# Block 0's second 256 rows of x, transposed by DMA instead of TensorE

## Chip, cores and metric

The kernel runs on one core of a Trainium2 chip. The metric is device microseconds (us) of one execution; the median of 8 runs of the kernel before is 290.55 us (289.83 to 290.69).

## What is computed

A two-layer dense block with a squared ReLU between the layers, all in bf16:

```
B, S, D, F = 1, 2048, 576, 4608
h = einsum("bsd,df->bsf", x, w1) + b1
r = where(h > 0, h, 0)
h = r * r
out = einsum("bsf,fd->bsd", h, w2) + b2
```

## The kernel before

The 2048 rows of x are four blocks of 512. The first layer wants x transposed (D on the partitions), and w1's columns are cut into 36 tiles of 128, so the hidden layer of one block is 36 tiles of 128x512, each summed in a PSUM bank, passed through ReLU with bias on ACT (L193) and squared on DVE (L195). The second layer (from L315) runs after all four blocks and is not touched.

For blocks 1 to 3 the transposed x comes straight from memory by DMA transposes (`load_xT`, L270), and one step of the first layer (`a_step`, L212) makes two tiles by 18 matmuls of half the array's rows. Block 0 begins differently, since TensorE would otherwise have nothing to do. Its x is loaded as plain rows, 128 at a time (`load_x`, L92, named x0 to x3 here, on SP's queue), and its first six tiles of w1 come in four chunks of 128 rows (`load_quad`, L95, named q0 to q3, on ACT's queue) and a rest of 64 rows (`load_rest`, L104). `transpose_tile` (L174) turns pieces of x on TensorE into a PSUM bank, and ACT or DVE copies them into `xT[0]`. `full_mm(j, n, c)` (L226) multiplies chunk c into six PSUM banks for the n*128 rows that begin at row 128*j: six matmuls of 128 or 256 columns each. The written order, L219 to L253, weaves 20 transposes and 13 calls of `full_mm` so that a matmul is there while the next piece of x or w1 is on its way.

After that come b1's transpose (L255), six matmuls on the rest of w1 (L260), and then the steps of the first layer for block 0 (L299), beginning with step 3. Its weights, and those of the steps after it, were put in SP's queue behind x and the rest of w1 (L117 to L119): two loads for every one, two or four steps, in the order of use. The next transposes (L275) stand behind these.

`manual_schedule` keeps the program's order on every engine. Two things are inserted by the program: `issue_at_barrier` (L123) lifts those first DMAs of SP and ACT that wait for nothing into the start-up block, the first two of each queue ahead of its drain and the others behind it. And each DMA on SP or ACT uses one of eight semaphores in turn; so a DMA is issued only once the DMA eight places earlier, of the two queues together, has landed. The first reuse is by `load_rest`; it waits for q0.

Of the kernel before, what the change touches and what calls it, by code (L numbers as in the profile page):

```python
# [17 lines left out]
def kernel(  # L18
# [9 lines left out]
    nc = tc.nc  # L28
    P = 128
    H = 64  # L30
    x2 = x.flatten_outer_dims()
    out2 = out.flatten_outer_dims()
    S, D = x2.shape
# [6 lines left out]
    NC = D // P  # L40
    NH = D // H
    DM = NC * P
    SB = 512
    NSB = S // SB
    RT = SB // P
    HALF = SB // 2
# [23 lines left out]
    def early(n):  # L70
        at[0] += n
        assert at[0] <= NFT * D
        return w2_sb[:, at[0] - n:at[0]]


    xT = [early(XW).rearrange("p (w s) -> p w s", s=SB) for b in range(NSB - 1)]
    xT3 = xpool.tile([P, NH, SB], BF16, name="xT3", tag="xT3")
    xT.append(xT3[:])
    xs = early(RT * D).rearrange("p (j c) -> p j c", c=D)
    qn = early(NC * G * P).rearrange("p (c f) -> p c f", c=NC)  # L80
    qr = early(GP * P)
    pairs = [(i, GP + i) for i in range(GP)] + [(G + i, G + NJ - GP + i) for i in range(NJ - GP)]
# [9 lines left out]
    def load_x(eng, j):  # L92
        eng.dma_start(out=xs[:, j, :], in_=x_view[:, j, :])

    def load_quad(eng, c):  # L95
        eng.dma_start(out=qn[:, c, :], in_=w1[c * P:(c + 1) * P, 0:G * P])
# [9 lines left out]

    b1T = const.tile([P, NFT], FP32, name="b1T")
    warm = const.tile([P, 1], FP32, name="warm")
    for j in range(RT):
        load_x(nc.sync, j)  # L110
        load_quad(nc.scalar, j)
    nc.scalar.activation(out=warm[:], in_=nc.const_aps.tensor(1.0, [P, 1], FP32), func=ACT.Relu)  # L112
    for h in range(2):
        load_rest(nc.sync, h)
# [8 lines left out]
    def issue_at_barrier(nc):  # L123
        entry, body = nc.main_func.blocks[:2]
        for engine in (mybir.EngineType.SP, mybir.EngineType.Activation):
            mine = [i for i in body.instructions if i.engine == engine and not isinstance(i, mybir.InstNoOp)]
            n = 0
            while isinstance(mine[n], mybir.InstDMACopy) and not mine[n].has_wait():
                n += 1
            assert n >= RT  # L130
            for k, i in enumerate(mine[:n]):
                wanted = mybir.InstDrain if k < 2 else mybir.InstEventSemaphore
                at = next(k for k, i in enumerate(entry.instructions) if i.engine == engine and isinstance(i, wanted))
                body.instructions.remove(i)
                entry.instructions.insert(at, i)

    nc.at_finalize(issue_at_barrier)


# [28 lines left out]
    def copy_psum(eng, dst, src):  # L168
        if eng is nc.scalar:
            nc.scalar.copy(out=dst, in_=src)  # L170
        else:
            nc.vector.tensor_copy(out=dst, in_=src)  # L172

    def transpose_tile(j, c, n, eng):  # L174
        cols = slice(j * P, (j + 1) * P)
        tp = psum.tile([P, n, P], BF16, name="tp", tag="bank")
        for k in range(n):
            d0 = (c + k) * P if c < NC else D - P
            nc.tensor.transpose(tp[:, k, :], xs[:, j, d0:d0 + P], ident[:])  # L179
        c0 = c if c < NC else 7  # L180
        copy_psum(eng, xT[0][:, c0:c0 + n, cols], tp[:])
        if c == NC:
            copy_psum(eng, xT[0][0:H, 8, cols], tp[H:P, 0, :])
# [35 lines left out]
    V, A = nc.vector, nc.scalar  # L219
# [6 lines left out]
    def full_mm(j, n, c):  # L226
        cols = slice(j * P, (j + n) * P)
        for q in range(G):
            nc.tensor.matmul(bk0[q][:, cols], lhsT=qn[:, c, q * P:(q + 1) * P], rhs=xT[0][:, c, cols],  # L229
                             start=(j == 0 and c == 0), stop=False, skip_group_check=True)  # L230
# [3 lines left out]
    transpose_tile(1, 2, 2, A)  # L234
    full_mm(0, 1, 1)
    full_mm(1, 1, 0)
    transpose_tile(2, 0, 2, V)
    full_mm(1, 1, 1)
    transpose_tile(2, 2, 2, A)
    full_mm(0, 2, 2)  # L240
    transpose_tile(3, 0, 2, V)
    full_mm(2, 1, 0)
    full_mm(2, 1, 1)
    transpose_tile(3, 2, 2, A)
    full_mm(2, 1, 2)
    transpose_tile(1, NC, 1, V)
    full_mm(0, 2, 3)
    transpose_tile(2, NC, 1, V)
    full_mm(3, 1, 0)
    full_mm(3, 1, 1)  # L250
    transpose_tile(3, NC, 1, A)
    full_mm(3, 1, 2)
    full_mm(2, 2, 3)  # L253
    b1T_ps = psum.tile([P, P], BF16, name="b1T_ps", tag="bank")
    nc.tensor.transpose(b1T_ps[:], b1_rows[:], ident[:])  # L255
    nc.vector.tensor_copy(out=b1T[:], in_=b1T_ps[:, 0:NFT])
    for i in range(GP):
        for h in range(2):
# [117 lines left out]
```

## Time and profile before

| | |
|---|---|
| median of 8 runs | 290.55 us |
| the profiled execution | 290.01 us, of which the span of the profile is 288.2 us |
| PE busy | 284.5 us (99%) |
| DVE, ACT busy | 79.8 us (28%), 95.5 us (33%) |
| first step of the first layer begins (L209) | 11.14 us |
| second layer begins (L322) | 145.33 us |

Times in the profile are counted from the start of its span. The 1.8 us between span and execution are outside of what it shows. "SPq" and "ACTq" are the instruction queues that issue DMAs; the time shown for such a row is that of issuing, and "to landing" counts from the start of issue to the last of 16 completions. The names in a row leave numbers out: `w_sb` is the memory of w2, which holds `xT`, the plain x and the first chunks of w1 until w2 is loaded.

### The profile page before, as it was taken

The numbers are of one execution on the slowest core, as the hardware profiler recorded it, in microseconds if no ns is written. First come the engines' busy times: TensorE is split into PE (matmuls) and PEld (weight loads), VectorE is DVE, ScalarE is ACT, GpSimd is POOL, SyncE is SP. The second block draws the span as 40 slices with busy tenths as digits, with TensorE's granted clock in tenths as the row PEclk, the third lists the DMA queues.
The fourth block names the chain that finished last, engine by engine and source line by source line (L and its number), as shares of the span: only waits on it lengthen the run. The fifth ranks groups of instructions, "written<-read, shape, count | busy, mean of one in ns | idle before, by whom it ended". The sixth has DMA issues, their size and how long they took to land.

```text
span 288.2 us, 4883 instructions
## 1 busy us (share of the span) xinstructions
PE 284.5 (99%) x2097; PEld 135.1 (47%) x2108; DVE 79.8 (28%) x200; ACT 95.5 (33%) x154; POOL 1.5 (1%) x8
## 2 busy tenths in 40 slices
PE   9999999999999999999999999999999999999996
PEld 6644444444444444444445444444444444444454
DVE  2654444544444444444420011111100011111111
ACT  3676766666676666667620000000000000000000
POOL 2000000000000000000000000000000000000000
PEclk9999999999999999999999999999999999999999
DMA  8999999930400005200000000000000000000000
GB/s 242 182 202 204 196 140 227 281 105 0 125 0 2 1 2 156 92 0 2 0 3 18 20 20 20 23 20 9 12 23 20 20 20 23 20 20 22 23 20 20
DMA packets 35381, 18.31 MB, mean 64 GB/s; under 512 B 22804, under 2 KB 35360, under 8 KB 35360
## 3 DMA queue, kind: packets, MB, share of 16 engines
q1 hardware_dynamic: 34752, 17.21, 26.8%
q10 hardware_dynamic: 576, 0.79, 0.8%
q8 instruction: 16, 0.26, 0.4%
q14 instruction: 5, 0.04, 0.1%
q0 software_dynamic: 32, 0.01, 0.0%
HBM read 12.23 MB, written 2.36 MB: 51 GB/s over the span
## 4 chain that ended last, share of the span: by engine, by line
PE 97%; ACT 1%; issue 0%; DVE 0%
PE ph L209 47%; PE po L336 43%; PE pc L322 5%; PE ph L229 2%; ACT L112 0%; PE tp L179 0%; PE ph L260 0%; DVE o_sb L338 0%; ACT w_sb L170 0%; ACT warm L112 0%; PE b1T_ps L255 0%
## 5 line engine op out<-in xcount | busy, mean ns | idle before, releaser
L193 ACT ACTIVATE r<-ph,b1T 128x512 bf16<-128x512 f32 x144 | 90.7, 686 | 45.8 <-PE ph L209 45.0
L209 PE MATMUL ph<-w_sb,w1h 64*128 64x512 bf16 x918 | 99.2, 376 | 0.0
L209 PEld LDWEIGHTS <-w1h 64*128 64x128 bf16 x1242 | 60.4, 94 | 73.6
L336 PE MATMUL po<-w_sb,hT 128*128 128x512 bf16 x423 | 92.9, 379 | 0.5
L336 PEld LDWEIGHTS <-hT 128*128 128x128 bf16 x432 | 42.2, 98 | 51.2 <-issue 0.4
L195 DVE TENSOR_TENSOR hT<-r 128x512 bf16<-128x512 bf16 x108 | 45.8, 425 | 52.3 <-ACT r L193 51.9
L338 DVE TENSOR_TENSOR o_sb<-po,b_bc 128x512 bf16<-128x512 f32 (+2 forms) x17 | 11.2, 660 | 116.7 <-PE po L336 109.7
L209 PE MATMUL ph<-xT,w1h 64*128 64x512 bf16 x324 | 35.1, 376 | 0.0
L336 PE MATMUL po<-w_sb,w1h 128*128 128x512 bf16 (+2 forms) x178 | 31.2, 336 | 0.1
L336 PEld LDWEIGHTS <-w1h 128*128 128x128 bf16 x180 | 16.2, 98 | 15.3
L195 DVE TENSOR_TENSOR w1h<-r 128x512 bf16<-128x512 bf16 x36 | 15.3, 425 | 19.6 <-ACT r L193 19.6
L322 PE MATMUL pc<-hT,w_sb 128*64 128x512 bf16 x108 | 15.7, 379 | 0.0
L322 PEld LDWEIGHTS <-w_sb 128*64 128x64 bf16 x144 | 8.1, 110 | 7.6 <-issue 0.4
L322 PE MATMUL pc<-w1h,w_sb 128*64 128x512 bf16 x36 | 7.9, 379 | 0.0
L229 PE MATMUL ph<-w_sb 128*128 128x128 bf16 (+1 forms) x78 | 6.9, 246 | 0.0
L229 PEld LDWEIGHTS <-w_sb 128*128 128x128 bf16 x78 | 5.9, 106 | 0.2
L324 ACT ACTIVATE oc<-pc,b2T 128x512 bf16<-128x512 f32 x2 | 1.4, 687 | 13.7 <-PE pc L322 13.7
L332 DVE COPY o_sb<-oc 128x64 bf16<-128x64 bf16 x16 | 2.8, 172 | 9.2 <-DMA oc<-oc 9.2
L172 DVE COPY w_sb<-tp 128x128 bf16<-128x128 bf16 (+2 forms) x11 | 2.6, 242 | 6.4 <-PE tp L179 6.3
L170 ACT COPY w_sb<-tp 128x256 bf16<-128x256 bf16 (+2 forms) x6 | 2.0, 334 | 4.5 <-PE tp L179 4.5
L179 PE MATMUL tp<-ident,w_sb 128*128 128x128 bf16 x20 | 3.1, 259 | 0.1
L166 PE MATMUL wps<-one 128*128 128x512 bf16 x5 | 2.3, 629 | 0.4 <-DVE one L141 0.4
(26 smaller groups left out, 10.6 us busy)
## 6 DMA issues: line engine op xcount, KB each, us to landing
w_sb<-in_w_dram SPq DMA_DIRECT2D x2, 1728.0 KB, 8.9
out_dram<-o_sb SPq DMA_DIRECT2D x15, 144.0 KB, 1.8
w1h<-in_w_dram SPq DMA_DIRECT2D x14, 144.0 KB, 4.4
w_sb<-in_w_dram SPq DMA_DIRECT2D x2, 864.0 KB, 7.4
w1h<-in_w_dram SPq DMA_DIRECT2D x4, 288.0 KB, 6.4
w1h<-in_w_dram SPq DMA_DIRECT2D x2, 576.0 KB, 10.2
w1h<-in_w_dram SPq DMA_DIRECT2D x2, 432.0 KB, 6.9
w_sb<-in_w_dram ACTq DMA_DIRECT2D x4, 192.0 KB, 3.9
```

The lines of the kernel that those rows point to most:

```text
L166: nc.tensor.matmul(wps[:], lhsT=ones[:, 0:P], rhs=ones[:], start=(i == 0), stop=(i == NWARM - 1))
L170: nc.scalar.copy(out=dst, in_=src)
L172: nc.vector.tensor_copy(out=dst, in_=src)
L179: nc.tensor.transpose(tp[:, k, :], xs[:, j, d0:d0 + P], ident[:])
L193: nc.scalar.activation(out=r[:], in_=bk[:], func=ACT.Relu, bias=b1T[:, ft:ft + 1], scale=1.0)
L195: nc.vector.tensor_tensor(out=hT_of(b, ft), in0=r3, in1=r3, op=ALU.mult)
L209: nc.tensor.matmul(bk[h][:], lhsT=w1h[rows, c, j * P:(j + 1) * P], rhs=xT[b][rows, place(h, c), :], start=(i == 0), stop=(i == NH - 1))
L229: nc.tensor.matmul(bk0[q][:, cols], lhsT=qn[:, c, q * P:(q + 1) * P], rhs=xT[0][:, c, cols], start=(j == 0 and c == 0), stop=False, skip_g ...
L322: nc.tensor.matmul(pc[h * H:(h + 1) * H, :], lhsT=w2(ft, DM, D), rhs=hT_of(2 * pr + h, ft), start=(ft == 0), stop=(ft == NFT - 1))
L332: nc.vector.tensor_copy(out=o_sb[:, DM:D], in_=o_tr[pr][:, jj, h * H:(h + 1) * H])
L336: nc.tensor.matmul(po[:, 0:e - a], lhsT=hT_of(b, ft)[:, jj, :], rhs=w2(ft, a, e), start=(ft == 0), stop=(ft == NFT - 1))
L338: nc.vector.tensor_tensor(out=o_sb[:, a:e], in0=po[:, 0:e - a], in1=b2_bc[:, a:e], op=ALU.add)
```

## The change

x2 and x3 are no longer loaded as plain rows. In their place in SP's queue stand two DMA transposes from memory, t0 and t1 here: t0 brings the 256 rows of x2 and x3 for the first 512 columns of D into `xT[0]`, t1 their last 128 columns, of which 64 are new and lie in the upper half of place 7; a copy on DVE puts those into place 8 as well. The 10 transposes of these rows on TensorE are gone, with their copies on DVE and ACT. The order of the matmuls is written anew: all four chunks meet the first 256 rows, and then each of the four chunks meets the second 256 rows in six matmuls of 256 columns. `issue_at_barrier` lifts transposes too; as before, SP's first four DMAs are lifted, two of them behind the drain.

```diff
-    xs = early(RT * D).rearrange("p (j c) -> p j c", c=D)
+    xs = early(RT // 2 * D).rearrange("p (j c) -> p j c", c=D)
...
-    for j in range(RT):
+    for j in range(2):
         load_x(nc.sync, j)
-        load_quad(nc.scalar, j)
+    for c in range(NC):
+        load_quad(nc.scalar, c)
+    late = slice(HALF, SB)
+    nc.sync.dma_start_transpose(out=xT[0][:, 0:NC, late], in_=x2[late, 0:DM])
+    nc.sync.dma_start_transpose(out=xT[0][:, 7, late], in_=x2[late, D - P:D])
...
-            while isinstance(mine[n], mybir.InstDMACopy) and not mine[n].has_wait():
+            while isinstance(mine[n], (mybir.InstDMACopy, mybir.InstDmaTransposeAnt)) and not mine[n].has_wait():
...
     full_mm(1, 1, 0)
-    transpose_tile(2, 0, 2, V)
     full_mm(1, 1, 1)
-    transpose_tile(2, 2, 2, A)
+    transpose_tile(1, NC, 1, V)
     full_mm(0, 2, 2)
-    transpose_tile(3, 0, 2, V)
-    full_mm(2, 1, 0)
-    full_mm(2, 1, 1)
-    transpose_tile(3, 2, 2, A)
-    full_mm(2, 1, 2)
-    transpose_tile(1, NC, 1, V)
     full_mm(0, 2, 3)
-    transpose_tile(2, NC, 1, V)
-    full_mm(3, 1, 0)
-    full_mm(3, 1, 1)
-    transpose_tile(3, NC, 1, A)
-    full_mm(3, 1, 2)
-    full_mm(2, 2, 3)
+    for c in range(NC):
+        full_mm(2, 2, c)
     b1T_ps = psum.tile([P, P], BF16, name="b1T_ps", tag="bank")
     nc.tensor.transpose(b1T_ps[:], b1_rows[:], ident[:])
+    nc.vector.tensor_copy(out=xT[0][0:H, 8, late], in_=xT[0][H:P, 7, late])
     nc.vector.tensor_copy(out=b1T[:], in_=b1T_ps[:, 0:NFT])
```

## The prediction

> **What bounds the kernel now.** I read the busy shares first, then the chain that ended last, then the first 12 us in order of time, then the DMAs behind them.
>
> ```profile
> PE 284.5 (99%) x2097; PEld 135.1 (47%) x2108; DVE 79.8 (28%) x200; ACT 95.5 (33%) x154; POOL 1.5 (1%) x8
> ...
> PE 97%; ACT 1%; issue 0%; DVE 0%
> ```
>
> The first line gives busy time by engine, the second the chain of waits by engine. TensorE is never free and is the chain, so a microsecond counts if it comes off TensorE's own stream, and only then. The chain in order of time shows the stretch that the change touches (start, length, what):
>
> ```profile
> 3.48 0.20 ACT warm L112
> 3.68 0.27 ACT w_sb L170
> 3.95 0.04 issue
> 3.99 0.58 PE tp L179 x4
> 4.58 0.99 PE ph L229 x12
> 5.57 0.11 PE tp L179 x2
> ...
> 9.50 0.99 PE ph L229 x12
> 10.49 0.06 PE b1T_ps L255
> 10.55 0.75 PE ph L260 x6
> 11.30 134.03 PE ph L209 x1242
> ```
>
> From 3.99 on nothing but TensorE stands in it: transposes (tp) and matmuls (ph) follow each other without a gap up to 145 us. In the starts of single matmuls, 128 columns take 107 ns until 5.12 and 56 ns afterwards, 256 columns 109 ns. All ten removed transposes run after 5.12.
>
> The timeline of the queues gives the issues (start, length), and the lines of single DMAs the landings:
>
> ```profile
> 0.00 1.92 SPq L93 DMA_DIRECT2D w_sb<-in_x_dram  x4
> ...
> 0.12 1.95 ACTq L96 DMA_DIRECT2D w_sb<-in_w_dram  x4
> ...
> 2.91 1.19 SPq L105 DMA_DIRECT2D w_sb<-in_w_dram  x2
> ...
> 4.14 16.57 SPq L100 DMA_DIRECT2D w1h<-in_w_dram  x20
> ```
>
> q3 is issued at 1.61 and lands 5.2 later, at 6.8; q2 at 1.25, landing at 5.5; x2 lands at 5.2, x3 at 6.5. The first use of x3 begins at 6.51, so x3 just comes in time now, and q3 has 1.1 us to spare before its first use at 7.90. The DMAs are not idle (window, PE, PEld, DVE, ACT, POOL busy, clock, DMA share, GB/s):
>
> ```profile
> 0.00:5.00 5.00, 4.54 (x26) 2.84 (x27) 1.16 (x6) 2.12 (x4) 1.51 (x8) 1.00 0.79 247
> 5.00:11.10 6.10, 6.10 (x87) 5.43 (x86) 1.97 (x8) 1.47 (x5) 0.00 (x0) 1.00 1.04 213
> ...
> 40.00:42.00 2.00, 2.00 (x22) 0.88 (x18) 1.49 (x5) 1.27 (x2) 0.00 (x0) 1.00 0.87 55
> ...
> 44.00:46.00 2.00, 2.00 (x22) 0.92 (x20) 0.91 (x3) 1.27 (x2) 0.00 (x0) 1.00 0.99 207
> ```
>
> The last two are stretches in which DMA transposes ran almost alone: 207 GB/s in one, 55 in the other.
>
> What is known of issuing a transpose (min, median, max in ns):
>
> ```profile
> L326 SPq DMA_TRANSPOSE oc<-oc x2: 1191/1198/1206, 154.0 to 161.7; - x2
> ...
> L273 SPq DMA_TRANSPOSE w_sb<-in_x_dram x4: 2422/4985/9015, 20.8 to 39.3; - x4
> L273 SPq DMA_TRANSPOSE xT<-in_x_dram x2: 2062/2347/2632, 43.7 to 46.4; - x2
> ```
>
> The first moves 128 KB with nothing else under way and lands after 2.4 us. The others move 512 KB each and are issued behind other transfers; their landing takes 4.9 to 11.6 us.
>
> **What the Trainium skill says.** "DMA: Bandwidth & Descriptors", section "Issuing engines are not separate DMA queues": DMAs of all queues run on the same 16 DMA engines and interleave. The trace agrees: x on SP and q on ACT land in turn (x1 3.3, q1 4.2, x2 5.2, q2 5.5, x3 6.5, q3 6.8). So t0 does not only have to arrive, it also pushes q2 and q3. The same page, "Why a DMA increments its semaphore by 16 and not by 1": only the full count says that all has landed. For q3, 15 of the 16 completions are in at 6.10 and the last at 6.78, so the slowest DMA engine decides. "Advanced Engine Details and Errata", "X-Bar Transpose (TRN2)": transposes are as fast as regular DMAs. Here 207 GB/s against 247 for plain rows of 1152 and 1536 B, and once 55; I use the measured rates.
>
> **The change part by part.**
>
> *TensorE.* Ten transposes of 56 ns go: 0.56. Of 60 matmuls of 128 columns 36 become 18 of 256: 36 x 55.9 - 18 x 109 = 0.05. Together 0.61 us, if TensorE never waits. Nothing before 5.12 moves: x0, q0, x1, q1 keep their places, and ACT's start (table load from 2.19) sets 3.99 as before. At nothing: the copies that go from DVE and ACT (both idle there for most of the time), and the new copy on DVE, behind t1 and ahead of b1's copy; it has from t1's landing to about 9.8.
>
> *The new due times.* full_mm(1,1,1) begins at 5.40, the last transpose of x1 at 5.74, full_mm(0,2,2) at 5.80, full_mm(0,2,3) at 5.80 + 6 x 0.109 = 6.45, the second 256 rows at 7.10. So q2 is wanted at 5.80 (landed 5.5 before), q3 at 6.45 (6.8 before; now wanted 1.45 earlier), t0 at 7.10, t1 at 9.7. If all are in time, L209 begins at 10.53 instead of 11.14.
>
> *DMA work.* x2 and x3 were 295 KB; t0 and t1 are 262 + 66 = 328 KB. At 247 and 213 GB/s that is 1.19 and 1.54 us, so 0.35 more; from the single packets (16 of 1152 B at 51 ns for each DMA engine against 80 of 256 B at 18 ns) 0.62 more. So all of q3, t0 and t1 is in at about 6.8 + 0.35 to 0.6 = 7.2 to 7.4, t1 being last. q3 can land earlier than before, if the engines alternate between small pieces of t0 and q, since less of t0 than of x2 and x3 then comes first: 6.0 at best. If t0 goes as one piece ahead of q2, its 1.15 us at each engine against x2's 0.41 puts q3 at 7.5. I take 6.65, since the slow engine remains, and so a wait of 0.2 at full_mm(0,2,3). t0 then is wanted at 7.3, and I expect it between 6.4 and 7.3.
>
> *SP's queue.* Behind t0 and t1 stand load_rest and the 20 loads of L100, then all else of SP. Issue of a transpose, by a line through 1.19 for 128 KB and 2.06 for 512 KB, is 0.9 + 0.29 for each 128 KB: t0 1.5, t1 1.05; both end at about 3.7 instead of 1.9. The bounds are 1.0 + 0.5 (in proportion to 2.06, with a floor) and 2.1 + 1.2. load_rest thus moves from 2.91 to 3.7 (2.9 to 4.5), as do all after it. Two waits are added: by the semaphores, the third load of L100 waits for t0 and the sixth for t1, where x2 (landed at 5.2) and q3 (6.8) were waited for. Cover: the rest of w1 landed at 7.7 and is wanted at 9.9; step 3's weights at 8.5, wanted at 10.5; step 4's at 10.1, wanted at 12.5; step 5's at 12.9, wanted at 14.4. A delay of 0.8 with 0.6 less time leaves all in time; a step takes 1.94 us of TensorE, and the DMAs bring its weights in some 1.45, so the cover grows afterwards. The start-up barrier isn't held: SP's part in it is its drain at 0.92, ahead of t0.
>
> *Sum.* -0.61 + 0.2 = -0.4 us: a span of 287.8, an execution of 289.6 against the profiled 290.01. That execution was 0.54 under the median; from the median the forecast is 290.55 - 0.4 = 290.15 us.
>
> **The rivals.**
>
> *Full gain.* q3 lands at 6.4 or before, t0 by 7.1: -0.6, 289.95. For it: small pieces of t0 in front of q. Against: the slow DMA engine, which has put q3 at 6.8.
>
> *The transpose is held by plain transfers (the slower side).* t0 shares the DMA engines with q1 to q3, which no transpose in this trace does; behind plain loads the first of L273 went badly: between 27.75 and 29.5, while the last packets of the loads before it were still running on some engines, it got 482 of its 2048 packets through, and then 280 in every 0.25 us. That looks as if the engines had to go forward together. Add 40 to 42 us at 55 GB/s. If t0's 262 KB crawl from x1's landing at 3.3 at 55 GB/s, they take 4.8 us and land at 8.1; with q held up too, 8.8. TensorE then waits 1.7 at the second 256 rows: +1.1, 291.65. It becomes slower than before from a landing at 7.7, by more than 0.2% from 8.3. Against it: 207 GB/s or more in most stretches, and x1's completions are only 0.4 us apart over the engines, so these reach t0 nearly together.
>
> *SP is held.* Each transpose of L273 behind another one ended its issue about when its predecessor landed. If t1 does the same with t0, its issue ends at about 6.5, load_rest lands at 9, and step 3's second load at 11.0 to 11.5, wanted at 10.5 to 10.9. That eats the gain: -0.4 + 0.6 = +0.2, 290.75, up to +0.9. Against it: at the end of each such issue about 95 to 130 packets for each DMA engine were still to go; t0 and t1 are 80 together, so a limit on these would not bite.
>
> **How the numbers follow.** The likeliest case, 0.45: some of the gain, 290.0 to 290.4. Full gain 0.22. Held transpose 0.20. SP held 0.13, about half of it over the line. A measurement of this kernel tells about 0.2% (0.58 us) from no change: faster means under 289.97, slower over 291.13. Faster: 0.22 and 0.05 of the likeliest case's lower end, 0.27. Slower: 0.20 and 0.07, 0.27. Same: 0.46. The range reaches from a little below the full gain, 289.75, to the held transpose, 291.5; by itself the likeliest case has 289.9 to 290.5.
>
> **What would show it.** Right: the chain has four calls' 24 matmuls of 256 columns in one piece of 2.6 us, a wait of 0 to 0.4 for q3 just before full_mm(0,2,3), L209 beginning at 10.6 to 10.9, t0's issue 1.0 to 2.1 us long. Wrong: PE idle over 0.6 us, or a wait for t0 by name (then the held transpose); a wait at L209 for w1h (SP held); 128-column matmuls at 107 ns after 5.2, which would mean that the clock came up later, a thing I have left as it is.

## The result, and the profile after

The changed kernel takes 292.16 us (median of 11 runs, 291.34 to 294.01) against 290.45 us before (32 runs, 289.64 to 291.04). The ratio is 1.0067, 95% interval 1.0053 to 1.0081: slower by two thirds of a per cent. The profiled execution took 294.03 us with a span of 292.2 us, 4.02 us more than the profiled execution before.

The page of the changed kernel has these shares, engines first and then the chain that ended last:

```profile
PE 285.9 (98%) x2069; PEld 135.1 (46%) x2080; DVE 78.9 (27%) x197; ACT 94.2 (32%) x150; POOL 1.5 (1%) x8
...
PE 96%; DMA 3%; ACTq 0%; issue 0%; DVE 0%
```

TensorE has 28 instructions fewer and yet 1.4 us more of busy time, and a DMA now stands in the chain where none stood before. The chain of waits in order of time (start, length, what) shows which:

```profile
1.61 7.79 DMA w_sb<-in_w_dram
9.39 0.05 issue
9.44 5.06 PE ph L233 x30
14.50 0.06 PE b1T_ps L248
14.55 0.76 PE ph L254 x6
15.31 134.03 PE ph L213 x1242
```

The DMA is q3: issued at 1.61 as before, landed at 9.39 instead of 6.78. L213 is what was L209. Its 1242 matmuls take 134.03 us as before, but begin at 15.31 instead of 11.30 (in the chain, which counts from modelled ends; the first of them starts at 15.15 instead of 11.14). So the whole loss of 4.01 us lies ahead of 15.31. The 30 matmuls of 256 columns at L233 take 5.06 us; at 109 ns each they would take 3.3.

The timeline of TensorE for the same stretch (start, length, engine, line, what, and in brackets the idle time before it and what ended it):

```profile
4.35 0.61 PE L183 MATMUL tp<-ident,w_sb 128*128 128x128 bf16 x4 [0.43 <-DMA w_sb<-in_x_dram]
...
9.44 5.06 PE L233 MATMUL ph<-w_sb 128*128 128x256 bf16 x30 [2.23 <-DMA w_sb<-in_w_dram]
```

There is a short wait for x1, which landed at 4.30 instead of 3.26, and a long one for q3. Taken from the starts of single matmuls (the brackets count from modelled ends), the first is 0.64 us where it was 0.29 before (there for ACT's copy, not for x1), the second 2.40. The transposes themselves, t0 at 9.76 and t1 at 10.53, landed in time for what then was late anyway.

SP's queue (start and length of the issues) is as the prediction had it:

```profile
1.11 1.33 SPq L114 DMA_TRANSPOSE w_sb<-in_x_dram  x1
2.49 1.23 SPq L115 DMA_TRANSPOSE w_sb<-in_x_dram  x1
3.86 1.19 SPq L105 DMA_DIRECT2D w_sb<-in_w_dram  x2
```

What went wrong lies in what the DMA engines moved. Each line is one microsecond: window, length, then busy time of PE, PEld, DVE, ACT and POOL, clock, DMA share, GB/s. First the kernel before:

```profile
4.00:5.00 1.00, 1.00 (x10) 1.00 (x10) 0.29 (x1) 0.37 (x1) 0.00 (x0) 1.00 1.04 361
5.00:6.00 1.00, 1.00 (x20) 1.00 (x18) 0.28 (x1) 0.00 (x0) 0.00 (x0) 1.00 0.89 282
```

And the changed kernel:

```profile
4.00:5.00 1.00, 0.65 (x7) 0.66 (x8) 0.22 (x1) 0.01 (x1) 0.00 (x0) 1.00 1.88 146
5.00:6.00 1.00, 1.00 (x13) 1.00 (x12) 0.07 (x1) 0.36 (x1) 0.00 (x0) 1.00 0.49 62
...
7.00:8.00 1.00, 0.21 (x2) 0.00 (x0) 0.05 (x1) 0.00 (x0) 0.00 (x0) 1.00 1.44 123
8.00:9.00 1.00, 0.00 (x0) 0.00 (x0) 0.00 (x0) 0.00 (x0) 0.00 (x0) 1.00 1.33 109
```

In these two microseconds, in which most of q2 and q3 came in before, the DMA engines moved 643 KB then and 208 KB now. The single packets say the same: 218 of q's 512 packets of 1536 B started after t0's first packet (3.54 us). They took 171 ns each on average, against 74 for those ahead of it; from 4.5 to 5.5 us only 20 of them started on all 16 engines together.

The last part of the loss is in the clock column of the same view:

```profile
7.00:9.40 2.40, 0.21 (x2) 0.00 (x0) 0.05 (x1) 0.00 (x0) 0.00 (x0) 0.99 1.29 125
9.40:12.80 3.40, 3.36 (x16) 2.41 (x17) 0.22 (x1) 0.00 (x0) 0.00 (x0) 0.50 0.97 156
12.80:16.00 3.20, 3.20 (x31) 2.07 (x30) 1.38 (x4) 1.09 (x2) 0.00 (x0) 1.00 1.01 203
```

After the wait for q3 the clock is at half for 3.4 us, and 256 columns take 213 ns instead of 109. The Trainium skill, "TensorE: Matmul & The Clock Gate", section "What's actually happening", says that the clock falls to half after an idle window of about 3.4 us, and that these windows run freely. Here a wait of 2.40 us was enough, and the half clock lasted 3.413 us. It happened in 3 of 13 executions of this kernel (294.03, 293.71 and 294.01 us); the other ten kept the full clock and took 291.34 to 292.29.

So the 4.01 us of the profiled execution are: 0.36 by which the wait for x1 ends later (4.35 against 3.99); 0.24 by a clock that first came up later (5.95 against 5.12, so the stretch at half clock from there is 1.60 us instead of 1.13, and half of the difference is lost); 2.40 by the wait for q3; 1.67 by the half clock after it (half of the 3.34 us of it in which TensorE works); less the 0.61 that TensorE no longer does. The sum is 4.06, 0.05 over what is measured. Without the half clock after the wait the loss would be 2.3 us, or 292.4 us in all, about the upper end of the other ten.

### The profile page after: what moved, and what is told of

It is laid out like the page before. It is cut to its first block, busy times and chain, and to the rows that moved or that the text cites. A ratio compares the mean times of both kernels' runs of the same rounds, so it can differ in the third digit from the quotient of the medians.

```text
span 292.2 us, 4819 instructions
## 1 busy us (share of the span) xinstructions
PE 285.9 (98%) x2069; PEld 135.1 (46%) x2080; DVE 78.9 (27%) x197; ACT 94.2 (32%) x150; POOL 1.5 (1%) x8
## 4 chain that ended last, share of the span: by engine, by line
PE 96%; DMA 3%; ACTq 0%; issue 0%; DVE 0%
PE ph L213 46%; PE po L330 42%; PE pc L316 5%; DMA w_sb<-in_w_dram 3%; PE ph L233 2%; ACTq L96 0%; PE ph L254 0%; DVE o_sb L332 0%; ACTq L354 0%; PE b1T_ps L248 0%
## 5 line engine op out<-in xcount | busy, mean ns | idle before, releaser
L213 PE MATMUL ph<-w_sb,w1h 64*128 64x512 bf16 x918 | 99.2, 376 | 0.0
L213 PEld LDWEIGHTS <-w1h 64*128 64x128 bf16 x1242 | 60.4, 94 | 73.6
L213 PE MATMUL ph<-xT,w1h 64*128 64x512 bf16 x324 | 35.1, 376 | 0.0
L233 PE MATMUL ph<-w_sb 128*128 128x256 bf16 (+1 forms) x60 | 8.3, 315 | 2.2 <-DMA w_sb<-in_w_dram 2.2
L233 PEld LDWEIGHTS <-w_sb 128*128 128x128 bf16 x60 | 6.5, 126 | 3.7 <-DMA w_sb<-in_w_dram 2.5
L176 DVE COPY w_sb<-tp 128x128 bf16<-128x128 bf16 (+2 forms) x7 | 1.5, 233 | 5.2 <-PE tp L183 5.1
L183 PE MATMUL tp<-ident,w_sb 128*128 128x128 bf16 x10 | 1.5, 298 | 0.4 <-DMA w_sb<-in_x_dram 0.4
```

The source lines that it names most:

```text
L213: nc.tensor.matmul(bk[h][:], lhsT=w1h[rows, c, j * P:(j + 1) * P], rhs=xT[b][rows, place(h, c), :], start=(i == 0), stop=(i == NH - 1))
```

## The experiments

The theory after the comparison, A: a DMA transpose and plain loads of another queue hold each other up while much of both is under way, and q3 is the load that pays for it. Its rivals, set against it in the expectations below: the order of the matmuls, the smaller packets, SP's queue, the clock.

**q2 and q3 in the transposes' own queue.** q2 and q3 go to SP's queue ahead of t0, so that no plain load stands beside t0 in another queue.

```diff
-    for c in range(NC):
+    for c in range(2):
         load_quad(nc.scalar, c)
+    for c in range(2, NC):
+        load_quad(nc.sync, c)
```

> The changed kernel, but q2 and q3 go into SP's queue ahead of t0 and t1, so that no plain load of another queue runs beside the transposes (q0 and q1 stay on ACT). Theory A (a transpose and plain loads of another queue hold each other): q3 lands by 6.8 us instead of 9.4, t0 by 7.5, TensorE waits under 0.5 us in the first layer's start, time 289.5 to 290.3 us; ACT's table load also starts earlier, worth at most 0.3 of it. Theory B (the transposes are simply slow or heavy work for the DMA engines, whoever runs beside them): q3 early, but t0 lands at 9 or later, a wait of 1.5 to 2.5 us at the second 256 rows, time 291.5 to 292.5.

Measured: 289.97 us (17 runs) beside 290.25 before, ratio 0.9987 (0.9978 to 0.9996). q3 landed at 5.27, t0 at 6.59, t1 at 6.77, and TensorE waited for none of them:

```profile
4.53 1.77 PE ph L235 x18
6.30 0.06 PE tp L185
6.35 3.93 PE ph L235 x36
```

The same bytes and the same two transposes, in one queue one after the other, came in 3 to 4 us earlier than in the profile of the changed kernel. So it isn't the transposes by themselves that make q3 late.

**The control for it.** The kernel before with q2 on SP behind x2 and q3 on SP behind x3, without any transposing DMA in this stretch:

```diff
-        load_quad(nc.scalar, j)
+        load_quad(nc.scalar if j < 2 else nc.sync, j)
```

> The kernel before with q2 and q3 on SP's queue behind x2 and x3 in turn, no DMA transpose in the start: what the freed ACT queue alone brings to e1_q_ahead. If e1's gain comes from the transposes taken off TensorE (0.6 us) this is within 0.3 us of the kernel before, 290.0 to 290.6. If it comes from ACT's earlier table load, this gains as much as e1 did, 289.7 to 290.0.

Measured: 289.82 us (21 runs) beside 290.35, ratio 0.9985 (0.9977 to 0.9994). So this pair shows no gain from the transposes: moving two loads from ACT's queue to SP's does as much without them. In both profiles of this pair the wait ahead of x1's transposes is gone as well; before, ACT's start had set that point, and its table load now begins at 1.40 instead of 2.19. The two profiles can't show the 0.61 us either: their clocks came up at 6.00 and 4.26, which alone is worth 0.9 us to the control.

**The order of the matmuls alone.** The loads of before, and all four chunks meet the first 256 rows ahead of x2's transposes:

```diff
     full_mm(1, 1, 0)
-    transpose_tile(2, 0, 2, V)
     full_mm(1, 1, 1)
-    transpose_tile(2, 2, 2, A)
+    transpose_tile(1, NC, 1, V)
     full_mm(0, 2, 2)
+    full_mm(0, 2, 3)
+    transpose_tile(2, 0, 2, V)
+    transpose_tile(2, 2, 2, A)
     transpose_tile(3, 0, 2, V)
     full_mm(2, 1, 0)
     full_mm(2, 1, 1)
...
-    transpose_tile(1, NC, 1, V)
-    full_mm(0, 2, 3)
```

> The kernel before with the new order of matmuls alone: all four chunks meet the first 256 rows before any of the second 256, x2 and x3 still loaded as rows and transposed on TensorE. Theory A: q3 lands at 6.8 as before and is wanted at 6.45, a wait of 0.3 to 0.4 us, time 290.5 to 291.0. Theory C (the order is the cost, because q3 is wanted early): most of the loss is here too, 291.5 or more.

Measured: 290.82 us (22 runs) beside 290.25, ratio 1.0024 (1.0015 to 1.0032). q3 landed at 6.66 and did not make TensorE wait. What it waits for instead stands in its chain of waits:

```profile
7.54 0.12 PE tp L179 x2
7.66 0.02 issue
7.68 0.30 DVE w_sb L172
7.99 0.04 issue
8.03 0.27 PE tp L179 x2
```

That is a copy out of PSUM which nothing covers any more, 0.43 us with the start of the next transposes. The changed kernel has no such transposes, so this number can't be subtracted from its loss. What the run does show is that an early q3, due at about 6.5, is no trouble while its queue is undisturbed: 6.66, next to the 6.65 that I took.

**Small packets without transposing.** Plain loads in pieces of 256 B take the place of t0 and t1. They bring the same bytes in packets of the same size, but leave out the transposition of these 256 rows.

```diff
-    nc.sync.dma_start_transpose(out=xT[0][:, 0:NC, late], in_=x2[late, 0:DM])
-    nc.sync.dma_start_transpose(out=xT[0][:, 7, late], in_=x2[late, D - P:D])
+    for r in range(2):
+        rs = slice(HALF + r * P, HALF + (r + 1) * P)
+        nc.sync.dma_start(out=xT[0][:, 0:NC, rs], in_=x2[rs, 0:DM].rearrange("p (c k) -> p c k", k=P))
+    nc.sync.dma_start(out=xT[0][:, 7, late].rearrange("p (r k) -> p r k", k=P),
+                      in_=x2[late, D - P:D].rearrange("(r p) k -> p r k", p=P))
```

> The changed kernel with plain loads in place of t0 and t1, of the same rows into the same places in as many pieces of 256 B; what is left out is the transposition of these rows. Theory A: q3 lands at 6.5 to 7.3 us, TensorE waits under 0.8 us, time 289.8 to 290.6. Theory B' (the number of small pieces and the bytes hold q2 and q3): q3 lands at 8.5 or later and the time stays at 291.5 to 292.5.

Measured: 290.34 us (22 runs) beside 290.25, ratio 1.0004 (0.9994 to 1.0013). Its chain of waits begins so:

```profile
1.61 5.82 DMA w_sb<-in_w_dram
7.43 0.05 issue
7.48 3.45 PE ph L236 x30
```

q3 lands at 7.43, 0.65 later than before the change, and TensorE waits 0.47 us for it (and 0.33 for q2 before that): that much the small packets do. But the DMA engines don't stand still (windows as above):

```profile
4.00:5.00 1.00, 1.00 (x11) 0.99 (x10) 0.29 (x1) 0.37 (x1) 0.00 (x0) 1.00 0.99 268
5.00:6.00 1.00, 1.00 (x16) 1.00 (x13) 0.00 (x0) 0.00 (x0) 0.00 (x0) 1.00 1.11 307
```

575 KB come in where the transposes left 208. Here 299 packets of q started beside the small pieces, more than in the changed kernel, and took 78 ns each instead of 171. What holds q3 beyond 7.43 is the transposing, then, and not the size or the number of packets.

**Where in SP's queue.** Three kernels leave q0 to q3 on ACT and put the transposes further back: behind one half of `load_rest`, behind both, and behind both and the two loads for step 3.

```diff
     late = slice(HALF, SB)
-    nc.sync.dma_start_transpose(out=xT[0][:, 0:NC, late], in_=x2[late, 0:DM])
-    nc.sync.dma_start_transpose(out=xT[0][:, 7, late], in_=x2[late, D - P:D])
...
     for h in range(2):
         load_rest(nc.sync, h)
+    nc.sync.dma_start_transpose(out=xT[0][:, 0:NC, late], in_=x2[late, 0:DM])
+    nc.sync.dma_start_transpose(out=xT[0][:, 7, late], in_=x2[late, D - P:D])
```

(this is the second of the three). Expected of the first, the second and the third:

> The changed kernel with the first of the two loads of w1's rest (load_rest, h = 0) moved ahead of t0 in SP's queue, the second left behind t1: t0's issue begins some 0.6 us later, at about 1.7, when q0 to q3 have run 0.6 us longer by themselves. This sets an overlap between the changed kernel's (218 packets of q still to start after t0's first packet, 291.9) and that with both loads ahead (15 packets, 289.9). Theory A (a transpose and the plain loads of another queue hold each other up, the more of both is outstanding): 80 to 190 packets of q after t0's first, their mean duration above 90 ns, q3 at 7.0 to 8.6, time 290.2 to 291.7. Theory B (it is only the place of t0 in the order of SP's queue that counts, whatever is outstanding on the other queue): as the changed kernel, q3 at 8.3 to 9.4, time 291.8 to 292.2, or as the one with both loads ahead, 289.9, with nothing between.

> The changed kernel with t0 and t1 behind the rest of w1 in SP's queue, so that t0 is issued at 2.9 when q0 has landed, and is beside q2 and q3 for a shorter time. Theory A: q3 lands at 6.3 to 7.3, t0 at 7.0 to 8.0, TensorE waits 0.2 to 1.0 us, time 290.0 to 291.0. If the transposes hold plain loads as soon as they meet at all, q3 lands after 8 and the time is over 291.3.

> The changed kernel, but t0 and t1 stand in SP's queue behind the rest of w1 and step 3's two loads, so that q3 has landed before they move. Theory A: q3 lands at 6.8 as before the change, t0 runs beside nothing of another queue and lands at 8.0 to 9.0, TensorE waits 0.3 us for q3 and 0.5 to 1.5 us for t0, time 290.2 to 291.3. Theory B: t0 lands after 10.5, time over 292.

Behind one half: 290.60 us (14 runs) beside 290.37, ratio 1.0010 (0.9998 to 1.0021). q3 landed at 6.36, t0 at 7.77, and TensorE waited 0.52 us for x1, 0.35 for q2 and 0.67 for t0. The time lies between the others, as A had it and B not; but A was wrong on how: q's packets took 68 ns beside t0, and q3 was not held.

Behind both: 289.91 us (22 runs) beside 290.35, ratio 0.9986 (0.9978 to 0.9994). q3 at 6.18, t0 at 7.24:

```profile
2.94 4.30 DMA w_sb<-in_x_dram
7.24 0.04 issue
7.28 2.78 PE ph L233 x24
```

A wait of 0.39 for t0 is left, and the kernel is faster than before all the same.

Behind both and step 3's loads: 291.33 us (9 runs) beside 290.25, ratio 1.0046 (1.0027 to 1.0065). t0 is issued at 4.60, behind step 3's two loads, and lands 4.87 us later, at 9.47 instead of the 8.0 to 9.0 expected:

```profile
4.60 4.87 DMA w_sb<-in_x_dram
9.47 0.04 issue
9.51 2.78 PE ph L235 x24
```

q3 was in at 6.12, so what this pays for is t0 being late, 2.39 us of waiting, and the clock fell to half in 2 of 9 executions (293.12 and 293.24). Issued at 1.11 the transposes hold q3, at 4.60 they are late themselves; at 2.94 they fit.

**Only q2 moved.** q2 stands on SP ahead of t0, q3 stays on ACT:

```diff
     for c in range(NC):
-        load_quad(nc.scalar, c)
+        load_quad(nc.sync if c == 2 else nc.scalar, c)
```

> The changed kernel with q2 alone moved to SP ahead of t0; q3 stays on ACT, beside the transposes. Theory A: the hold is smaller but there, q3 lands at 6.5 to 8.5 and t0 later than in e1_q_ahead (6.6), at 7.0 to 8.5; TensorE waits 0.3 to 1.5 us, time 290.3 to 291.5, between e1_q_ahead and the changed kernel. If only the number of bytes ahead of q3 counts, q3 lands by 6.5 and the time is that of e1, 289.7 to 290.1.

Measured: 289.59 us (11 runs) beside 290.35, ratio 0.9973 (0.9964 to 0.9982), the lowest of all. My theory was too strong here: q3 landed at 5.37, and its 80 packets that started after t0's first took 69 ns each, against 66 of the ones before. One q beside the transpose is not held. The run was made again, together with a control in which the kernel before has q2 on SP between x2 and x3:

```diff
-        load_quad(nc.scalar, j)
+        load_quad(nc.sync if j == 2 else nc.scalar, j)
```

> The changed kernel with q2 alone on SP ahead of t0, again and on the same chip as its control. No part left out. Theory A and B both: 289.4 to 289.9, no wait for q3, t0 or t1, and q3 and t0 in at 5.0 to 7.0; they differ in the distance to the control: A at least 0.4 us below it, B within 0.3.

> The kernel before (x2 and x3 as plain rows, its own order of transposes and matmuls) with q2 alone moved to SP's queue, between x2 and x3: the control for the changed kernel with q2 alone on SP, 289.59. Both have one load less in ACT's queue; only the other has t0 and t1. Theory A (where nothing waits, the transposes' 0.61 us of TensorE comes off the time, and the queue gives at most 0.2 by an earlier start of ACT): 290.1 to 290.4, at least 0.4 us above the other run of this call. Theory B (the gain is the freed queue, as with q2 and q3 on SP): 289.5 to 289.9, within 0.3 us of it.

Measured: 289.77 us (14 runs), ratio 0.9984 (0.9971 to 0.9997), and for the control 290.34 us (13 runs), ratio 1.0004 (0.9993 to 1.0016), both beside 290.39. The 0.57 us between them is what theory A there gives, and next to the 0.61 of the prediction. It isn't a clean measure of it: the control's profile has a wait of 0.19 us of its own, for q2, which lands at 6.23 there instead of 5.48, and the two intervals overlap by 0.0004 (that of the run before it doesn't reach the control's). The chain of the repeated run has no wait from 2.7 us on:

```profile
2.69 0.53 PE tp L183 x5
3.22 0.69 PE ph L233 x6
3.91 0.43 PE tp L183 x4
4.33 1.78 PE ph L233 x18
6.11 0.06 PE tp L183
6.17 3.93 PE ph L233 x36
```

and the last row is what the changed kernel was meant to look like: the two calls for q2 and q3 and the four for the second 256 rows in one piece of 36 matmuls, 109 ns each.

**The wait for q3 filled.** Ten matmuls of 512 columns on constants after `full_mm(0, 2, 2)` keep TensorE at work while it waits:

```diff
     full_mm(0, 2, 2)
+    fill = bank("fill")
+    for i in range(10):
+        nc.tensor.matmul(fill[:], lhsT=ones[:, 0:P], rhs=ones[:], start=(i == 0), stop=(i == 9))
     full_mm(0, 2, 3)
```

> The changed kernel with ten 512-column matmuls on ones into a spare PSUM bank ahead of full_mm(0,2,3), 2.2 us at full clock, to fill TensorE's wait for q3. Theory A (q3 lands about 9.4, and in some executions the clock falls to half after the wait): no execution has a granted clock of 0.994, none is over 293; the median is 291.6 to 292.2, the profile has q3 landing at 8.5 to 9.5 still. If q3 usually lands much earlier than in the profiled execution, the filler costs up to 2.2 us more and the median is 292.5 to 294.

Measured: 292.01 us (5 runs, 291.98 to 292.37) beside 290.35, ratio 1.0063 (1.0051 to 1.0075). The chain:

```profile
6.16 0.05 issue
6.20 0.83 PE ph L233 x6
7.03 2.18 PE fill L246 x10
9.21 3.27 PE ph L233 x30
```

q3 landed at 8.37, so the filling is 0.65 us or more too long, and costs that. What it shows: the matmuls after it run at full clock in the profile (30 in 3.27 us), and none of the five executions shows the half clock. Against 3 of 13 without the filling (4 of 17 with the run below), five are too few to call the difference shown.

**The changed kernel again,** nothing altered, to see an execution at full clock:

> The changed kernel once more with nothing altered, to see the order of events in an execution whose TensorE clock is full throughout. Theory A (the wait for q3 is there in every execution, and the half clock after it only in some): a wait of 1.3 to 2.4 us for q3, q3 landing at 8.3 to 9.4 and t0 at 8.6 to 9.8, a_step's first matmul at 12.9 to 13.5 where the clock stays full, and a median of 291.5 to 292.3. Theory B (the half clock is itself the cause of the loss and the wait is small without it): no wait over 0.8 us and a time under 290.8 where the clock is full.

Measured: 290.87, 292.27, 292.57 and 293.85 us, median 292.42 beside 290.37, ratio 1.0087 (1.0062 to 1.0112). 293.85 is again one with the clock at half. The profiled execution is the fastest of all of this kernel, 290.87:

```profile
1.62 6.25 DMA w_sb<-in_w_dram
7.87 0.05 issue
7.92 3.45 PE ph L233 x30
```

q3 landed at 7.87, t0 at 8.28. The wait for q3 is 0.73 us, less than A had expected of every execution, because TensorE was late itself: its clock came up at 6.50 (5.12 in the profile before). The loss against the profile before, 0.87 us at the first step, is 0.12 by a later start, 0.6 by the later clock, 0.73 by q3, less 0.61. So how long the hold lasts differs from execution to execution: q3 at 9.39, 8.37 and 7.87 in three profiles of this order of loads.

The dose in one table, from the single packets (q packets of ACT's queue that started after the first packet of t0 or of the small pieces, their mean duration before and after that, and landings):

| kernel | q packets beside | ns, before and beside | q3 | t0 | ratio |
|---|---|---|---|---|---|
| changed | 218 | 74, 171 | 9.39 | 9.76 | 1.0067 |
| changed again | 199 | 78, 114 | 7.87 | 8.28 | 1.0087 |
| filled wait | 192 | 81, 155 | 8.37 | 8.66 | 1.0063 |
| half of the rest ahead | 110 | 87, 68 | 6.36 | 7.77 | 1.0010 |
| only q2 moved | 80 | 66, 69 | 5.37 | 6.73 | 0.9973 |
| only q2 moved, again | 77 | 75, 67 | 5.56 | 6.98 | 0.9984 |
| behind the rest | 15 | 71, 65 | 6.18 | 7.24 | 0.9986 |
| q2 and q3 ahead | 0 | 65, none | 5.27 | 6.59 | 0.9987 |
| plain small pieces | 299 | 65, 78 | 7.43 | none | 1.0004 |

Up to 110 packets of plain load beside the transposes these packets aren't slowed; from 192 on they are. Between lies a step that the runs don't place more closely. Nor do they separate the number from the time: t0's first packet started at 3.54 to 3.84 in the first three kernels and at 4.09 or later in the others with transposes.

Plain load need not stand in another queue to be slowed. `load_rest`, in SP's own queue behind t1, has packets that took 65 ns on average with q2 and q3 ahead, 17 of its 128 over 100 ns; behind the plain small pieces it was 40 ns and none. That costs nothing here, since it is wanted late.

## Why the prediction was wrong

- **Which side.** Forecast 290.15 in a range of 289.75 to 291.5, measured 292.16. Slower had a chance of 0.27, and the mechanism was among the rivals: "the transpose is held by plain transfers", 0.20, priced at 291.65. The one that came is this rival, but with a different item in front.
- **The step that failed** is "I take 6.65" for q3's landing, with 7.5 as its upper bound. Measured 9.39, 8.37 and 7.87. The working there added the bytes and packets of q, t0 and t1 at the rates of plain loads (213 GB/s, 18 ns for 256 B), and let the engines alternate between them; in this sum, that each could slow the other's packets stands at nothing. For plain load the bound of 7.5 holds: with plain pieces of the same size q3 landed at 7.43. The transposing costs what lies beyond, 0.4 to 2 us.
- **The rival's own price** let t0 crawl at 55 GB/s from 3.3 and land at 8.1 to 8.8, with q3 merely in its train. t0 landed at 9.76, 8.66 and 8.28, so its size was about right; but the earliest thing wanted was q3, due at 6.45, 0.65 us ahead of t0. In the profile of the changed kernel the wait was therefore longer, 2.40 us, than the 1.7 priced there; repeated, with q3 at 7.87, it was 0.73.
- **The evidence against that rival** was weak. Its transposes that ran at 207 GB/s had no plain loads beside them, and so said nothing on this case; the 482 packets in 1.75 us came from a stretch that had both, in one queue. The Trainium skill, "Advanced Engine Details and Errata", section "X-Bar Transpose (TRN2)", says that transposes are as fast as regular DMAs. In one queue, behind the plain loads, t0's 262 KB were in 1.32 us after q3 (199 GB/s), where in the control without transposes q3's 196 KB came 0.63 us after x3 (312 GB/s): slower, but in time. Beside 190 or more packets of another queue t0 is far later, and slows that queue too.
- **Nothing before 5.12 moves** was wrong by 0.36 us: x1 landed at 4.30 instead of 3.26. Whether t0 did this is not shown: its first packets started at 3.54, beside x1's last ones, but x1 landed at 4.03 too where t0 began only at 4.41 (half of the rest ahead).
- **The clock** was named as left out. In the profile it cost 0.24 at the start and 1.67 after the wait. The second part is not in the median, since most executions kept the full clock.
- **TensorE's saving** of 0.61 has its parts right: 36 matmuls of 256 columns in 3.93 us without a gap where nothing waits. As time it showed once (0.57 between the runs with q2 moved) and once not (none between those with q2 and q3 moved). Why not stays open. In the profiles the clock first came up anywhere from 3.27 to 6.50 us, and half of the stretch until then is lost each time; and the three runs in which TensorE has the same work and waits for none of these loads (289.59, 289.77 and 289.97) already lie 0.38 us apart.
- **SP's queue** was right: t0's issue 1.33 (1.5 forecast), t1's 1.23 (1.05), `load_rest` at 3.86 (3.7). "SP is held" fell: t1's issue did not wait for t0. The third load of L100 did wait for it, as the semaphores said, and was issued at 9.78, with 3 us of cover left before it is wanted.

What is not shown is why the two hold each other. That the 16 engines have to go through a transpose together, so that one engine busy with plain packets stops the others, would fit the microsecond with 20 packets of q. It would also fit the stretch of 55 GB/s that the prediction read as transposes almost alone: an instruction fetch of 8 KB began there at 39.71 and took 1.87 us, and 19 transposing packets that started at 39.81 to 39.83 took 1.51 to 1.52 us each instead of 18 ns. But a second stall at 41.66, of 22 packets and 0.9 us, has no other packet beside it, and no run here tested the idea.

## What to carry to other kernels

A transposing DMA is not another load of so many bytes: before it goes into one queue, look at what plain load of other queues is still under way when its first packet starts, and ask which of these loads is wanted first. Put it behind those loads in their own queue, or late enough that few of their packets are left; the same two transposes cost 0.67% here, and with one load of 196 KB moved ahead of them the kernel gained 0.27%, and 0.16% when repeated. And set the gain beside the plain alternative: moving two loads to the other queue gave 0.15% without any transpose.

## What the hardware showed besides

- A wait of about 2.4 us can drop TensorE's clock to half for 3.4 us. It happened in 6 of 26 executions of the two kernels whose profiles have such a wait (the changed one, in one of its two profiles, and the one with the transposes behind step 3's loads), each time 1.6 to 2.0 us over the median of the others; in the kernels whose longest wait in the profile is under 0.7 us it happened in none.
- The same wait need not do it. With the transposes behind step 3's loads the profile has a wait of 2.39 us, from 7.12 to 9.51, and the clock stays full. The full clock there began at 5.12 and lasted 286.72 us, which is 84 times 3.413; counted in such steps, a boundary lies at 8.53 and cuts the wait into 1.41 and 0.98 us. In the changed kernel 2.32 of the 2.40 us lie in one step, from 5.95 to 9.36. So where the wait falls seems to matter as much as its length; these are two profiles, and no run tested it.
